# A gated mix of linear attention and softmax attention: Strassen groups over eight banks instead of six, v's split weights loaded back piece by piece, and kv's first weights loaded one per unit of v

## The chip, the cores and the metric

One NeuronCore of a Trainium2 chip runs the whole program. The metric is the device time of one execution in microseconds (us); lower is better. Five engines work side by side: PE (TensorE) does the matrix products and writes its sums to eight PSUM banks of 128 x 512 fp32; DVE (VectorE), ACT (ScalarE) and POOL (GpSimd) read and write banks and on-chip tiles; SP (SyncE) does nothing but issue transfers between memory and on-chip tiles. Each engine takes its instructions strictly in the order written, and waits at an instruction until all that it needs is there.

## The reference

Two attention blocks of 32 heads of 32 columns each see the same x (2048 rows, 1024 columns). A is linear attention, B is softmax attention, and a gate per row mixes them:

```
phi = lambda t: where(t > 0, t + 1, exp(t)) + 1e-6
A:  q, k, v = x @ A_wqkv         pq, pk = phi(q), phi(k)
    kv = pk^T v   z = sum(pk)    o = (pq kv) / (pq z + 1e-6)     a = o @ A_wo
B:  q, k, v = x @ B_wqkv         p = softmax(q k^T / sqrt(32))   b = (p v) @ B_wo
g = sigmoid(sum(x * gate_w))
result = g * a + (1 - g) * b
```

## The kernel before

**Three products for one.** A fp32 product is made of three faster ones. A tile t is split into a high part (ACT copies t into the fast type, L294) and a low part (DVE or POOL subtracts the high part from t, L295). The helper `three` then adds hi x hi (L153), hi x lo (L156) and lo x hi (L158) into one bank. So a line L153 in the profile is the first matmul of a triple and is the one that waits when a bank isn't free; L156 is the first that needs a low part.

**The stages.** B's v, q and k come first. The 2048 rows of x are four column blocks of x transposed, taken as two pairs, J = 0 and J = 1. For each pair:

- *v's pass*, `v_pass(J, k, banks)`: half of v's columns for the pair's 1024 rows. All eight banks are open at once, one for each 128 rows; for k = 0..7 every bank gets one triple. At the end ACT copies the eight banks out (L358, `v_out`).
- *Eight Strassen groups*, `quad(J, f, side)`: each makes 256 columns of q or k for the pair, as seven products of 12 matmuls. A product goes to the next bank of a ring of `NQB` banks. The products are read like this: ACT copies product 0 to P1 (L467); DVE adds product 1 to it (L469); products 2, 3 and 4 stay in their banks until DVE has product 4, and then L476, L477 and L478 read products 4, 3 and 2 in this order; L482 and L483 read product 5; L486 reads product 6. Each of the four results is split (`store`) and its two parts go to memory (`qk_d`), issued by SP. Between the steps, `quad` calls `next(side)`: one step each of the work that goes beside it. This is `quad_weights` (sums of q's and k's weights for the next group and their split), `late_side`, `spill_rest` (split parts of x put aside in memory, `xs`), and `wo_parts` (the output weights, on POOL and its own queue, L502 to L531).

In the first pair, v's split weights lie in places of the ring `RINGW`, which the groups' weights then overwrite. So `store_wv` puts them into memory (`wv_d`), and `load_wv_again` brings them back for J = 1, in the last group of J = 0 (`change`). The other side work of `change` is the split of the next pair's x, whose tiles are loaded by `load_pair`.

During v's pass the sums and differences of x blocks that Strassen's scheme needs are made by DVE (`sides`, L375 to L378), into tiles that held the groups' results and from which the stores to `qk_d` were made.

**After the groups** (from 417 us) comes a plan: a table `T` of each engine's expected time decides which work is written next. The function `linear` writes chunks in units of 24 matmuls (one 128-row tile, k = 0..7, in `three`). The first chunk is the other half of B's v, 16 units; then come chunks of A's k and v together ("kv"), then q and o. Beside them run the softmax heads: maxima of scores (matmuls L1232, L1237 on DVE), scores and exponentials (L1374, L1377), products with v (L1524), to the end. A chunk's weights are loaded by `load_w` into raw tiles, put in the queue `coming_w`, and split into place by `split_w` (L839 is its ACT cast). For the chunk that follows, the first `LEAD_W` = 5 weights are loaded in the last unit but one (t == NT - 2).

**Queues.** Every transfer made by `dma` is issued by SP (L170), in the order written. A transfer that waits for a tile to become free, or for one to be written, holds all that are written behind it.

Of the kernel before, what the change touches and what calls it, by code (L numbers as in the profile page):

```python
# [21 lines left out]
C = 512  # L22
# [3 lines left out]
LEAD_W = 5  # L26
# [23 lines left out]
def kernel(  # L50
# [31 lines left out]
    def f32(ap):  # L82
        return ap.bitcast(F32)
# [83 lines left out]
    def dma(to, of):  # L167

        T["sp"] = max(T["sp"], T["pe"]) + DMA_ISSUE
        nc.sync.dma_start(to, of)  # L170
# [140 lines left out]
    for side in PLACES:  # L311
        side["X12"] = side["T4"]
    NQB = 6
    RINGW = [(16, 0), (16, 1), (17, 0), (17, 1), (19, 0), (19, 1), (14, 0), (14, 1), (20, 0), (20, 1), (15, 0),
# [313 lines left out]

    V_BANKS = [list(range(8)), [6, 7, 2, 3, 4, 5, 0, 1]]
    raws_q = [raw_a, raw_b]  # L630
# [5 lines left out]

    def load_wv_again(ks):
        for k in ks:
            for p in range(2):
                dma(f32(ring_w(v_ring(1, k), p)), wv_d[k][:, p * C:(p + 1) * C])  # L640

# [31 lines left out]
    for k in range(NK):  # L673
# [5 lines left out]
        if k + 4 < NK:  # L679
            load_block(k + 4)  # L680
        v_pass(0, k, V_BANKS[0], range(TPC) if k == 0 else None)
        if k % 2:
# [19 lines left out]
    load_quad(raw_b, 1)  # L702
    for t, to in zip((0, 1, 6, 2, 3, 4, 5, 7), v_outs[0]):
        v_out(0, t, bank[V_BANKS[0][t]], to)

    def change():

        load_wv_again(range(NK - 2))
        split_x(raw_x1[0], 1, 0, 0)
        yield  # L710
        load_wv_again([NK - 2])
        split_x(raw_x1[0], 1, 1, 0)
        yield
        load_wv_again([NK - 1])
        split_x(raw_x1[0], 1, 0, 1)
        yield
        split_x(raw_x1[0], 1, 1, 1)
        yield
        split_x(raw_x1[1], 1, 0, 2)
        split_x(raw_x1[1], 1, 1, 2)  # L720
        yield
        split_x(raw_x1[1], 1, 0, 3)
        split_x(raw_x1[1], 1, 1, 3)
        yield

    quads(0, lambda: load_pair(raw_x1[0], 1, 0), spill_rest(0), parts)
    load_pair(raw_x1[1], 1, 1)
    quad(0, QUADS - 1, change())
    for k in range(NK):
        v_pass(1, k, V_BANKS[1])  # L730
        if k == 0:
# [31 lines left out]
    for t, to in enumerate(v_outs[1]):  # L763
        v_out(0, 2 * TPC + t, bank[V_BANKS[1][t]], to)

# [270 lines left out]
    def linear():  # L1036
        extra = iter(())
        for n, (i, t) in enumerate(units):
# [18 lines left out]
            for k in range(NK):  # L1057
# [37 lines left out]
                if follow and t == NT - 2 and k == 0:  # L1095
                    yield lambda: None if mix_here or stores else 0.0
                if follow and t == NT - 2 and k < min(LEAD_W, NK):
                    coming_w.append(load_w(*follow, k, LEAD_W + 1))
# [819 lines left out]
```

## Time and profile before

| | |
|---|---|
| median of 3 runs | 2833.21 us (2830.22 to 2836.54) |
| the profiled execution | 2832.33 us, its span 2830.3 us, granted clock 0.997 |
| PE from 540 us to the end | 2282.73 us busy of 2290.30 |

The profile describes one execution. A busy share says how long an engine had something in hand, not whether anyone waited for it; what the end hangs on is seen where PE waits and for whom. These are the stages of the span: length, then busy time and number of matmuls or instructions of PE, PE's weight loads, DVE, ACT and POOL, then the granted TensorE clock (1.00 is full), the busy share of the DMA engines and the GB/s that they moved.

```profile
0.00:51.00 51.00, 49.89 (x217) 41.58 (x218) 40.07 (x66) 28.50 (x51) 0.71 (x6) 1.00 0.93 298
51.00:211.40 160.40, 153.01 (x664) 124.98 (x662) 134.70 (x168) 56.01 (x117) 89.89 (x122) 0.99 0.91 287
211.40:259.00 47.60, 46.54 (x192) 37.69 (x192) 36.19 (x57) 20.18 (x36) 0.00 (x0) 0.94 0.79 250
259.00:417.00 158.00, 153.88 (x674) 126.16 (x675) 121.67 (x173) 59.46 (x115) 54.53 (x70) 1.00 0.79 253
417.00:540.00 123.00, 117.41 (x519) 94.94 (x518) 63.77 (x94) 38.60 (x66) 52.37 (x58) 0.99 0.87 270
540.00:2830.30 2290.30, 2282.73 (x13619) 1618.51 (x13617) 1934.73 (x3189) 1435.88 (x2713) 1905.68 (x895) 1.00 0.48 137
```

The rows are v's first pass, the first pair's groups, v's second pass, the second pair's groups, v's chunk, and all the rest.

### The profile page before, as it was taken

What the parts mean: (1) busy time and instruction counts of PE and PEld (TensorE: products, weight loads), DVE (VectorE), ACT (ScalarE), POOL (GpSimd) and SP (SyncE); (2) the same over time, 40 slices, a digit from 0 to 9 for tenths busy, and PEclk for the clock granted to TensorE, in tenths of its full rate; (3) what the DMA queues carried; (4) which work ended last, traced back from release to release, by engine and by line L of the source; (5) the groups of instructions that cost most, each with busy time, mean ns of one, the idle gap of its engine ahead of it and who ended that gap; (6) DMA issues with size and microseconds to landing.
All of it is one profiled execution on the core that took longest, in us unless ns stands there. A gap on an engine that the chain in (4) does not pass through costs nothing.

```text
span 2830.3 us, 47031 instructions
## 1 busy us (share of the span) xinstructions
PE 2803.5 (99%) x15880; PEld 2043.9 (72%) x15880; DVE 2331.1 (82%) x3745; ACT 1638.6 (58%) x3095; POOL 2103.2 (74%) x1150
## 2 busy tenths in 40 slices
PE   9999999999999999999999999999999999999999
PEld 8877788777776777667776777776676667666687
DVE  7886874788888888888888888888887888886688
ACT  5334332566676667666765666666666666666522
POOL 0660524599999998999899998989889988888000
PEclk9999999999999999999999999999999999999999
DMA  8997979633343434333433344556575554544774
GB/s 277 303 291 241 290 220 284 192 98 100 101 126 104 102 102 128 100 94 98 133 94 105 99 126 137 155 162 183 174 214 164 146 157 140 150 120 139 253 238 153
DMA packets 403340, 459.52 MB, mean 162 GB/s; under 512 B 106894, under 2 KB 234894, under 8 KB 401308
## 3 DMA queue, kind: packets, MB, share of 16 engines
q1 hardware_dynamic: 381084, 419.03, 48.7%
q0 software_dynamic: 22016, 37.50, 6.1%
q8 instruction: 126, 2.06, 0.3%
q14 instruction: 114, 0.93, 0.1%
HBM read 314.31 MB, written 127.66 MB: 156 GB/s over the span
## 4 chain that ended last, share of the span: by engine, by line
PE 85%; DMA 1%; issue 0%; DVE 0%; SPq 0%; ACT 0%; ACTq 0%; DVEq 0%
PE bank L1374 17%; PE bank L1232 16%; PE bank L1524 16%; PE bank L153 11%; PE bank L158 11%; PE bank L156 11%; PE bank L1296 1%; PE bank L1021 1%; PE bank L910 0%; DMA big<-ra 0%; DMA xh<-xs 0%; PE bank L1288 0%; SPq L170 0%; DMA big<-xs 0%; DMA extra<-in_a_wqkv 0%
## 5 line engine op out<-in xcount | busy, mean ns | idle before, releaser
L1459 POOL TENSOR_TENSOR big<-big,big 128x512 f32<-128x512 f32 (+2 forms) x694 | 1642.0, 2370 | 107.2 <-ACT big L1377 64.2
L1237 DVE TENSOR_REDUCE mx<-bank 128x1 f32<-128x512 f32 x2048 | 1314.6, 684 | 302.2 <-PE bank L1232 298.8
L1377 ACT ACTIVATE big<-bank 128x512 f32<-128x512 f32 x2048 | 1180.3, 602 | 429.6 <-PE bank L1374 364.1
L1374 PE MATMUL bank<-big,big 128*128 128x512 f32 x1888 | 741.7, 394 | 1.7 <-DMA big<-ml 1.7
L1232 PE MATMUL bank<-big,big 128*128 128x512 f32 x1888 | 739.6, 392 | 1.4 <-ACT big L1377 1.4
L153 PE MATMUL bank<-big,big 128*128 128x512 f32 x1576 | 619.1, 393 | 14.9 <-DVE mid L478 6.4
L156 PE MATMUL bank<-big,big 128*128 128x512 f32 x1576 | 617.0, 392 | 2.3 <-DVE big L295 1.8
L158 PE MATMUL bank<-big,big 128*128 128x512 f32 x1572 | 615.7, 392 | 0.0
L1524 PE MATMUL bank<-big,mid 128*32 128x512 f32 x4096 | 454.2, 593 | 0.0
L1374 PEld LDWEIGHTS bank<-big,big 128*128 128x128 f32 x1888 | 354.2, 188 | 125.9 <-issue 49.7
L1232 PEld LDWEIGHTS bank<-big,big 128*128 128x128 f32 x1888 | 354.6, 188 | 75.4 <-ACT big L1377 3.1
L153 PEld LDWEIGHTS bank<-big,big 128*128 128x128 f32 x1576 | 297.3, 189 | 83.8 <-issue 9.2
L156 PEld LDWEIGHTS bank<-big,big 128*128 128x128 f32 x1576 | 297.2, 189 | 65.5 <-DVE big L295 2.9
L158 PEld LDWEIGHTS bank<-big,big 128*128 128x128 f32 x1572 | 296.4, 189 | 64.5 <-DVE big L295 1.7
L1524 PEld LDWEIGHTS bank<-big,mid 128*32 128x32 f32 x4096 | 143.6, 110 | 264.4 <-issue 264.1
L1475 DVE TENSOR_TENSOR bank<-bank,big 128x512 f32<-128x512 f32 x364 | 252.2, 693 | 5.3 <-ACT big L1377 2.9
L294 ACT CAST big<-mid 128x512 fp32r<-128x512 f32 (+1 forms) x157 | 92.8, 618 | 116.2 <-DVE mid L1643 66.0
L295 DVE TENSOR_TENSOR big<-mid,big 128x512 fp32r<-128x512 f32 (+1 forms) x157 | 122.9, 799 | 43.9 <-ACT big L294 43.7
L1455 POOL TENSOR_TENSOR big<-big,big 128x1536 f32<-128x1536 f32 (+1 forms) x31 | 123.1, 3972 | 41.7 <-ACT big L1377 41.5
L153 PE MATMUL bank<-big,xh 128*128 128x512 f32 x376 | 147.2, 392 | 1.2 <-DMA xh<-xs 1.2
L158 PE MATMUL bank<-big,xh 128*128 128x512 f32 x376 | 147.0, 391 | 0.0
L156 PE MATMUL bank<-big,xh 128*128 128x512 f32 x376 | 146.8, 391 | 0.0
(163 smaller groups left out, 2122.9 us busy)
## 6 DMA issues: line engine op xcount, KB each, us to landing
big<-xs SPq DMA_DIRECT2D x288, 256.0 KB
big<-qk SPq DMA_DIRECT2D x690, 64.0 KB
xh<-xs SPq DMA_DIRECT2D x144, 256.0 KB
qk<-mid SPq DMA_DIRECT2D x128, 256.0 KB
big<-oA SPq DMA_DIRECT2D x84, 256.0 KB
xs<-big SPq DMA_DIRECT2D x64, 256.0 KB
oA<-mid SPq DMA_DIRECT2D x64, 256.0 KB
big<-big POOLq DMA_DIRECT2D x50, 256.0 KB, 5.8
```

The lines of the kernel that those rows point to most:

```text
L153: yield nc.tensor.matmul(ps, sh, mh_, start=(kt == 0), stop=False)
L156: yield nc.tensor.matmul(ps, sh, ml_, start=False, stop=(late and last))
L158: yield nc.tensor.matmul(ps, sl, mh_, start=False, stop=last)
L295: eng.tensor_sub(lo, src, f32(hi))
L1232: nc.tensor.matmul(bank[b], q[:, t % TPC * P:(t % TPC + 1) * P], k[:, j * C:(j + 1) * C], start=True, stop=True)
L1237: nc.vector.tensor_reduce(m[:, t, j:j + 1], bank[b], AX.X, ALU.max)
L1374: nc.tensor.matmul(bank[b], k[:, t * P:(t + 1) * P], q_cols(h, j), start=True, stop=True)
L1377: nc.scalar.activation(pr_t[i][:, j * C:(j + 1) * C], bank[b], AF.Exp, scale=SCALE)
L1455: nc.gpsimd.tensor_add(lacc[:, :qp], pr(0)[:, :qp], pr(1)[:, :qp])
L1459: nc.gpsimd.tensor_add(lacc[:, sl], lacc[:, sl], pr(t)[:, sl])
L1475: nc.vector.tensor_add(lacc[:, qp:] if t == NT - 1 else l_b[:, :n], l_b[:, :n], src)
L1524: nc.tensor.matmul(av_b[j * DH:(j + 1) * DH, :], v[:, t, :], pr(t)[:, j * C:(j + 1) * C], start=(t == 0), stop=(t == NT - 1))
```

## The change

Three edits, which leave what is computed as it is.

1. `NQB` is 8 instead of 6, and both of v's passes use the banks 0 to 7 in their order; `V_BANKS` goes. With six banks the last group of J = 0 ended in bank 1, and the second pass was given the order 6, 7, 2, 3, 4, 5, 0, 1; with eight it ends in bank 7. The first pass's banks are copied out in the order 0 to 7 instead of 0, 1, 6, 2, 3, 4, 5, 7.
2. v's split weights come back one place k at a time. A new stream `reload_wv` beside the groups waits for (8 - 2) x 7 + 1 = 43 steps and then loads k = 0 to 5, one per step, from group 6's second product on. `change` loads the last two. Before, `change` loaded k = 0 to 5 at group 7's first step, then k = 6, then k = 7.
3. After a chunk of v, the first five weights of the next chunk (kv) are loaded one in each of the units t = 10 to 14, at k = 0, instead of all five within t = 14, at k = 0 to 4.

```diff
-    NQB = 6
+    NQB = 8
...
-    V_BANKS = [list(range(8)), [6, 7, 2, 3, 4, 5, 0, 1]]
...
-    def load_wv_again(ks):
-        for k in ks:
-            for p in range(2):
-                dma(f32(ring_w(v_ring(1, k), p)), wv_d[k][:, p * C:(p + 1) * C])
+    def load_wv_again(k):
+        for p in range(2):
+            dma(f32(ring_w(v_ring(1, k), p)), wv_d[k][:, p * C:(p + 1) * C])
+
+    def reload_wv():
+
+        for _ in range((QUADS - 2) * NP + 1):
+            yield
+        for k in range(NK - 2):
+            load_wv_again(k)
+            yield
...
-    for t, to in zip((0, 1, 6, 2, 3, 4, 5, 7), v_outs[0]):
-        v_out(0, t, bank[V_BANKS[0][t]], to)
+    for t, to in enumerate(v_outs[0]):
+        v_out(0, t, bank[t], to)
 
     def change():
 
-        load_wv_again(range(NK - 2))
+        load_wv_again(NK - 2)
         split_x(raw_x1[0], 1, 0, 0)
         yield
-        load_wv_again([NK - 2])
+        load_wv_again(NK - 1)
         split_x(raw_x1[0], 1, 1, 0)
         yield
-        load_wv_again([NK - 1])
         split_x(raw_x1[0], 1, 0, 1)
...
-    quads(0, lambda: load_pair(raw_x1[0], 1, 0), spill_rest(0), parts)
+    quads(0, lambda: load_pair(raw_x1[0], 1, 0), reload_wv(), spill_rest(0), parts)
...
-        v_pass(1, k, V_BANKS[1])
+        v_pass(1, k, range(8))
...
-                if follow and t == NT - 2 and k < min(LEAD_W, NK):
+                if follow and kind == "v":
+                    if k == 0 and 0 <= t - (NT - 1 - LEAD_W) < LEAD_W:
+                        coming_w.append(load_w(*follow, t - (NT - 1 - LEAD_W), LEAD_W + 1))
+                elif follow and t == NT - 2 and k < min(LEAD_W, NK):
                     coming_w.append(load_w(*follow, k, LEAD_W + 1))
```

On PE, DVE, ACT and POOL the order of the instructions stays, but for ACT's copies of the first pass; it is the bank in each that changes. DVE in the second pair's first group, before (bank_238 to bank_245 are the banks 0 to 7; mid_226, mid_235 and mid_234 are P1, W2 and U2):

```order
L476 TENSOR_TENSOR mid_234<-bank_238,mid_226 128x512
L477 TENSOR_TENSOR mid_235<-bank_243,mid_234 128x512
L478 TENSOR_TENSOR mid_226<-bank_242,mid_235 128x512
L295 TENSOR_TENSOR mid_226<-mid_226,mid_232 128x512
L295 TENSOR_TENSOR big_222<-mid_225,big_222 128x512
L482 TENSOR_TENSOR mid_235<-bank_239,mid_235 128x512
L483 TENSOR_TENSOR mid_234<-bank_239,mid_234 128x512
```

And now:

```order
L476 TENSOR_TENSOR mid_234<-bank_242,mid_226 128x512
L477 TENSOR_TENSOR mid_235<-bank_241,mid_234 128x512
L478 TENSOR_TENSOR mid_226<-bank_240,mid_235 128x512
L295 TENSOR_TENSOR mid_226<-mid_226,mid_232 128x512
L295 TENSOR_TENSOR big_222<-mid_225,big_222 128x512
L482 TENSOR_TENSOR mid_235<-bank_243,mid_235 128x512
L483 TENSOR_TENSOR mid_234<-bank_243,mid_234 128x512
```

The group's products lay in the banks 2, 3, 4, 5, 0, 1, 2 and now lie in 0 to 6, so that the bank read by L478 is taken again eight products later and not six.

SP around the first pair's groups 6 and 7 (qk_... are the stores of a group's results, of which `_134` to `_143` belong to group 6 and `_150` to `_158` to group 7; wv_252 to wv_259 are v's split weights for k = 0 to 7; in_xT is x for the next pair):

```order
 L170 DMA qk_0_6_134<-mid_230 128x512
 L170 DMA qk_1_6_142<-mid_236 128x512
+L170 DMA big_614<-wv_252 128x512 x2
+L170 DMA big_221<-wv_253 128x512 x2
+L170 DMA big_221<-wv_254 128x512 x2
 L170 DMA qk_0_6_134<-mid_232 128x512
 L170 DMA qk_1_6_142<-mid_226 128x512
+L170 DMA big_222<-wv_255 128x512 x2
```

```order
 L170 DMA mid_228<-in_xT 128x512
-L170 DMA big_614<-wv_252 128x512 x2
-L170 DMA big_221<-wv_253 128x512 x2
-L170 DMA big_221<-wv_254 128x512 x2
-L170 DMA big_222<-wv_255 128x512 x2
-L170 DMA big_222<-wv_256 128x512 x2
-L170 DMA big_223<-wv_257 128x512 x2
+L170 DMA big_223<-wv_258 128x512 x2
 L170 DMA qk_0_6_150<-mid_230 128x512
 L170 DMA qk_1_6_158<-mid_236 128x512
-L170 DMA big_223<-wv_258 128x512 x2
```

Twelve loads went from between the x tiles and group 7's first stores to places among group 6's stores, ahead of the x tiles.

SP at the end of v's chunk (v_161 is a store of a finished unit, xs_ and xh are x put aside before and loaded again, in_a_wqkv are kv's weights):

```order
 L170 DMA big_210<-xs_3_82 128x512
 L170 DMA v_161<-mid_234 128x512
+L170 DMA mid_225<-in_a_wqkv 128x256 x2
```

```order
 L170 DMA big_210<-xs_7_86 128x512
 L170 DMA v_161<-mid_234 128x512
-L170 DMA mid_225<-in_a_wqkv 128x256 x2
+L170 DMA mid_229<-in_a_wqkv 128x256 x2
 L170 DMA mid_233<-in_xT 128x512
-L170 DMA extra<-in_a_wqkv 128x256 x2
-L170 DMA mid_227<-in_a_wqkv 128x256 x2
 L170 DMA big_210<-xs_7_70 128x512
 L170 DMA big_210<-xs_7_86 128x512
-L170 DMA mid_228<-in_a_wqkv 128x256 x2
 L170 DMA zrep<-in_xT 128x512
-L170 DMA mid_229<-in_a_wqkv 128x256 x2
```

The first weight (mid_225) now stands four units earlier, the other three that went from here one unit apart behind it; the fifth (mid_229) stays in the last unit but one.

More of the change, by code (lines that the diff above doesn't have):

```diff
@@ L680 @@
             load_block(k + 4)
-        v_pass(0, k, V_BANKS[0], range(TPC) if k == 0 else None)
+        v_pass(0, k, range(8), range(TPC) if k == 0 else None)
         if k % 2:
@@ L763 @@
     for t, to in enumerate(v_outs[1]):
-        v_out(0, 2 * TPC + t, bank[V_BANKS[1][t]], to)
+        v_out(0, 2 * TPC + t, bank[t], to)
     def load_v1(raws, ks):
```

## The prediction

> **What bounds the kernel now.** I read the page first, then the list of PE's waits, then the stretches in which those waits lie. The page says that the span is matmuls:
>
> ```profile
> span 2830.3 us, 47031 instructions
> PE 2803.5 (99%) x15880; PEld 2043.9 (72%) x15880; DVE 2331.1 (82%) x3745; ACT 1638.6 (58%) x3095; POOL 2103.2 (74%) x1150
> ```
>
> The change takes no matmul away, so it can win only what PE stands still or runs slowly. The list of waits (total us, times, longest) begins with these:
>
> ```profile
> PE bank L153 <- DVE mid L478: 6.4, 5, 2.5
> PE bank L153 <- DMA big<-xs: 3.2, 1, 3.2
> ```
>
> The rows quoted below place these and the next longest ones: all lie before 540 us, in the Strassen groups, between them and v's pass, and where v's chunk hands over to kv. What comes after 540 us is bound by PE itself, so what is won before reaches the end. The waits also cost clock. Windows (length, busy us and matmuls of PE, and so on; the granted clock is the third number from the right):
>
> ```profile
> 51.50:70.50 19.00, 19.00 (x85) 15.76 (x84) 12.25 (x20) 8.21 (x15) 1.25 (x2) 1.00 0.67 216
> 190.10:193.50 3.40, 3.12 (x7) 2.48 (x8) 2.67 (x3) 1.23 (x3) 3.30 (x5) 0.50 0.41 152
> 214.00:217.40 3.40, 3.40 (x9) 2.63 (x9) 2.90 (x5) 1.83 (x4) 0.00 (x0) 0.50 1.05 391
> 528.00:531.50 3.50, 3.50 (x11) 2.69 (x10) 1.38 (x2) 1.86 (x3) 0.45 (x1) 0.51 0.91 306
> ```
>
> At full clock 3.40 us hold 85 x 3.40/19.00 = 15 matmuls, at half clock 9: a slow stretch loses 6 x 0.224 = 1.4 us. There are four (two lie together, from 210.6). Each follows a wait of 2.5 us or more; after the shorter ones the clock stayed. So the most there is to win is 2830.3 - 2803.5 = 26.8 us of standing still and 5.6 us of clock.
>
> **Part 1: the eight banks.** A group is 84 matmuls, 19.0 us for PE. The five waits for L478 say that DVE reads product 2 late. The question is whether DVE is late because PE is, or by itself. The longest of DVE's own waits from 62 to 217 us, and L478 and PE at the start:
>
> ```profile
> DVE mid L295 <- ACT mid L294: 16.1, 22, 0.7
> L478 DVE TENSOR_TENSOR mid<-bank,mid x16: 691/691/692, 68.2 to 413.0; 128x512 f32<-128x512 f32 x16
> 51.03 0.39 PE L153 MATMUL bank<-big,big 128*128 128x512 f32 x1
> ```
>
> DVE waits there for ACT casts of DVE's own results, and for PE not once. Through the first pair's groups DVE sets its own pace: L478 comes at 68.2 us in group 0 and at 209.89 in group 7 (row below), 20.2 us apart on average against PE's 19.0. More banks cannot hurry it; they let PE run ahead until something else of DVE's stops it. That is the weights. DVE and PE around group 7 and the pass behind it:
>
> ```profile
> 189.55 0.69 DVE L478 TENSOR_TENSOR mid<-bank,mid 128x512 f32<-128x512 f32 x1
> 192.53 2.46 DVE L295 TENSOR_TENSOR big<-mid,big 128x512 fp32r<-128x512 f32 x1
> 193.13 1.30 POOL L531 TENSOR_TENSOR zrep<-zrep 128x512 f32<-128x512 f32 x1
> 209.89 0.69 DVE L478 TENSOR_TENSOR mid<-bank,mid 128x512 f32<-128x512 f32 x1
> 211.31 0.69 DVE L295 TENSOR_TENSOR mid<-mid,mid 128x512 fp32r<-128x512 f32 x1 [0.73 <-ACT mid L294]
> 216.35 0.69 DVE L486 TENSOR_TENSOR mid<-bank,mid 128x512 f32<-128x512 f32 x1
> 225.73 0.69 DVE L378 TENSOR_TENSOR mid<-xh 128x512 f32<-128x512 f32 x1 [5.22 <-DMA qk<-mid]
> 190.38 0.77 PE L153 MATMUL bank<-big,big 128*128 128x512 f32 x1 [2.53 <-DVE mid L478]
> 208.12 0.39 PE L158 MATMUL bank<-big,big 128*128 128x512 f32 x1
> 211.47 0.76 PE L153 MATMUL bank<-big,big 128*128 128x512 f32 x1 [2.96 <-DMA big<-wv]
> 219.59 0.39 PE L153 MATMUL bank<-big,big 128*128 128x512 f32 x1
> ```
>
> With eight banks PE, which begins group 0 at 51.03, starts group 7 at about 51.0 + 7 x 19.0 = 184 us and its product 2 two products, 5.4 us, later. The low half of that product's weights is the split at 192.53, done at 195.0. PE waits there instead, and has 10 matmuls and four products left (2.3 + 10.9 us): it ends the group at 208.2, where before it ended at 208.5 (the row at 208.12). I count the first pair's bank waits at nothing, then; their bounds go into the next sum.
>
> The split at 192.53 takes 2.46 us where the other DVE rows here take 0.69; POOL's subtraction `L531 zrep<-zrep` runs inside it. The Trainium skill, "SBUF — State Buffer", section "SBUF: two separate sides", says that a DVE instruction with two SBUF operands and a GpSimd one lock each other out of a shared port for the whole instruction. The trace agrees (2.46 against 0.69 us), and by that rule no number of banks shortens this chain.
>
> **Part 2: v's weights come back earlier.** The sixteen loads now issue from 204.5 us on, behind group 6's stores:
>
> ```profile
> 201.13 3.25 SPq L170 DMA_DIRECT2D mid<-in_xT  x4
> L170 SPq DMA_DIRECT2D big<-wv x16: 319/320/2086, 204.5 to 219.8; - x16
> 168.60:189.00 20.40, 19.26 (x85) 15.60 (x84) 18.59 (x21) 6.40 (x14) 13.04 (x18) 1.00 0.99 314
> 189.00:204.00 15.00, 13.62 (x53) 11.07 (x54) 12.24 (x14) 5.58 (x12) 10.01 (x14) 0.89 0.69 233
> 210.00:226.00 16.00, 14.03 (x50) 11.09 (x51) 9.13 (x15) 5.70 (x10) 0.00 (x0) 0.79 1.04 383
> ```
>
> Twelve of them move into 183 to 201 us. The last two columns (DMA share, GB/s) say that the stretch to 189 is full and the next has room. 12 x 0.262 MB at the 383 GB/s of the last row are 8.2 us of transfers. SP issues them one place per step, each right behind the product that frees its place, and PE, being ahead, has run that product. So the 2.96 + 0.50 us go. Next in line stands DVE: v's pass over k = 0 goes through banks 0 to 7, and banks 3, 6 and 7 hold group 7's products that L478, L483 and L486 read. L486 ends at 216.35 + 0.69 = 217.04, so the last bank of k = 0 starts at 217.1 where it started at 219.59: 2.5 us. PE comes to it through about 2 us of idling, near what halved the clock before; I put one slow stretch at one chance in two, 0.7 us. **Term 1: 2.5 - 0.7 = 1.8 us**; bounds -0.3 (two slow stretches) and 2.5.
>
> The Trainium skill, "TensorE: Matmul & The Clock Gate", section "HAM oscillation — how this bites in real kernels", lets the clock fall only after idling for a window of about 3.4 us. Here 2.53 us sufficed (0.50 in the row from 190.10), so the measurement decides; by the rule term 1 would be 2.5 us.
>
> The same loads did a second harm. Group 7's stores of q and k stood on SP behind them, and DVE's L378 (the row at 225.73), which overwrites a stored tile, waited 5.22 us. With the loads out of the way that store can go when its split is done (211.31 + 0.69 = 212.0) and L378 can run at 220.5. Behind it hang all of the pass's side matrices, the loads for them, ACT's copies of v and the split of T4 in the second pair's first group, so this chain comes 5.2 us earlier. PE itself comes 1.8 earlier, and so its waits on that chain go:
>
> ```profile
> 259.39 0.50 PE L153 MATMUL bank<-big,big 128*128 128x512 f32 x1 [0.88 <-ACT mid L358]
> 277.35 0.50 PE L156 MATMUL bank<-big,big 128*128 128x512 f32 x1 [1.07 <-DVE big L295]
> 279.75 0.50 PE L156 MATMUL bank<-big,big 128*128 128x512 f32 x1 [0.77 <-DVE big L295]
> 322.41 0.47 PE L153 MATMUL bank<-big,big 128*128 128x512 f32 x1 [0.44 <-DVE mid L478]
> 343.18 0.47 PE L153 MATMUL bank<-big,big 128*128 128x512 f32 x1 [1.45 <-DVE mid L478]
> 341.00:361.00 20.00, 18.55 (x83) 15.03 (x82) 16.46 (x26) 7.86 (x14) 0.00 (x0) 1.00 0.77 244
> ```
>
> **Term 2: 0.88 + 1.07 + 0.77 = 2.7 us**; bounds 0 (the chain stays where it is; then term 1 is swallowed too) and 2.7. The changed bank order alone also lets the first product follow the first of ACT's copies, not the third.
>
> **Term 3**: the second pair's bank waits, 0.44 + 1.45 = **1.9 us**. Here DVE has room (16.46 busy of 20.00 us), and two more products, 5.4 us, cover a lateness of 1.45. Bounds 0 (it comes back as a wait for weights, as in group 7) and 1.9.
>
> **Part 3: kv's first weights.** Where v's chunk ends:
>
> ```profile
> 520.33 0.99 SPq L170 DMA_DIRECT2D mid<-in_a_wqkv  x2
> 521.74 0.80 SPq L170 DMA_DIRECT2D big<-xs  x2
> 526.82 0.50 PE L153 MATMUL bank<-big,big 128*128 128x512 f32 x1 [3.24 <-DMA big<-xs]
> 536.77 0.62 ACT L839 CAST big<-extra 128x512 fp32r<-128x512 f32 x1 [0.99 <-DMA extra<-in_a_wqkv]
> 537.94 0.51 PE L1232 MATMUL bank<-big,big 128*128 128x512 f32 x1 [1.44 <-ACT big L1377]
> 480.00:512.00 32.00, 32.00 (x151) 26.69 (x150) 24.35 (x37) 11.07 (x20) 11.95 (x11) 1.00 0.89 274
> 516.00:537.00 21.00, 17.26 (x67) 12.97 (x65) 9.73 (x13) 7.60 (x13) 5.52 (x5) 0.92 0.91 296
> ```
>
> PE waits for x that SP issued behind kv's weights; then ACT's cast of the last weight waits for its load, an exponential stands behind the cast, and PE wants the exponential's bank. Of the ten loads of 0.131 MB that stand here together, eight move into the four units before (one pair stays). At 296 GB/s these are 0.44 us each. Eight moving out shorten the queue ahead of the last weight by 3.5 us, so PE resumes 3.5 earlier than 537.94. **Term 4: 3.5 us**, the two waits shrinking and the slow stretch at 528 going. Bounds 0 (the queue is as full in the units before, 0.89) and 3.24 + 1.44 + 1.4 = 6.1.
>
> Sum: 1.8 + 2.7 + 1.9 + 3.5 = 9.9 us. The profiled execution took 2832.33 us (its span 2830.3 and 2.0 around it), 0.9 below the median shown, within its runs' range. 2832.3 - 9.9 = **2822.4 us**.
>
> **Rivals.** *The chain behind L378 stays.* If the early loads make DVE or POOL wait elsewhere, all before 280 us stays DVE's: 1.9 + 3.5 = 5.4, 2826.9 us. For it: the full DMA before 189 us. Against it: room from 189 on. *kv's queue only moves.* With 0.89 in the units before, x comes late there: terms 1 to 3, 6.4, 2825.9 us. For it: 8 x 0.44 = 3.5 us of loads against 32 x 0.11 = 3.5 us of room. Against it: a pair of loads, 0.9 us, comes once per unit of 24 matmuls, 24 x 0.224 = 5.4 us. *The change does not do what it says*: every bank wait turns into a weight wait, in the second pair too, and the chain stays: 3.5 us, 2828.8. *Slower*: the twelve loads queue ahead of the four x tiles (the row at 201.13) that are split in group 7. Were their 8.2 us of transfers passed on whole, L486 would end at 225.2, PE be 5.6 late and 1.4 slower in clock, less terms 2 and 3 (4.6), and with kv's queue moved only: 2832.3 + 2.4 = 2834.7 us. It decides when those tiles land after 212 us, where DVE now splits them, behind the row at 211.31; they are issued from 201 on, and 189 to 204 has 15 x (1 - 0.69) = 4.6 us of room, so I hold it unlikely.
>
> **How the numbers follow.** The forecast 0.56, the first rival 0.13, the second 0.13, the third 0.10, slower 0.08. Its own bounds run from 2818 (term 4 at 6.1, no slow stretch) to 2826; with 3 us either way, the spread of the runs before, and the rivals' 2827 to 2829, the range is 2814 to 2830. A measurement of this kernel can tell 0.2%, 5.7 us, from no change: faster than 2827.5 are the forecast, the second rival and half of the first, 0.76; slower than 2838.9 is half of the slower case, where further waits join it, 0.04; no change is the rest, 0.20.
>
> **What would show it.** No wait for L478 by PE in the second pair; in the first pair a wait for L295 near 190 us in place of it, and PE at v's pass near 208 us as now. No wait for wv; waits for banks near 210 to 217. L378 without its 5.2 us, and none of the three waits between 259 and 280. Near 515 to 530 a wait for x under 2 us and a granted clock of 1.00. I am wrong if PE reaches the pass well before 208 us (then DVE followed PE after all), or if waits for xs appear between 480 and 515.

## The result: 6.9 us faster

| | before | changed |
|---|---|---|
| median | 2832.2 us (8 runs, 2827.87 to 2836.54) | 2825.31 us (8 runs, 2821.66 to 2829.28) |
| ratio | | 0.9977, 95% interval 0.9967 to 0.9988 |
| profiled execution | 2832.33 us, span 2830.3 | 2824.52 us, span 2822.7 |

The interval is a gain of 3.4 to 9.3 us. The forecast was 2822.4 us, 9.9 us faster than the profiled execution before; that one and the profiled one after are 7.8 apart.

The page of the changed kernel, first its span and the engines' busy time, and then the list of PE's waits (total us, times, longest):

```profile
span 2822.7 us, 47003 instructions
PE 2801.9 (99%) x15880; PEld 2043.3 (72%) x15880; DVE 2330.5 (83%) x3745; ACT 1638.2 (58%) x3095; POOL 2104.1 (75%) x1150
```

```profile
PE bank L153 <- DVE mid L486: 3.9, 1, 3.9
PE bank L153 <- DMA xh<-xs: 2.4, 2, 1.7
PE bank L153 <- ACT big L294: 2.3, 3, 1.2
PE bank L1382 <- DMA big<-ml: 2.2, 2, 1.6
PE bank L153 <- DVE mid L483: 1.5, 1, 1.5
PE bank L1240 <- ACT big L1385: 1.1, 1, 1.1
...
PE bank L153 <- DMA big<-xs: 1.0, 1, 1.0
PE bank L153 <- DVE mid L478: 0.4, 1, 0.4
```

The waits for L478 fell from 6.4 to 0.4 us and those for `wv` are gone. New on the list are L483 and L486, DVE's reads of the last two products of group 7: the next in line. (L1240, L1382 and L1385 are the lines 1232, 1374 and 1377 of before.)

Where the lead came from is best read by setting the start of the same matmul in both traces side by side. Both hold all 15880, so the nth of one is the nth of the other:

| place (us before) | PE's lead | gained there | forecast |
|---|---|---|---|
| v's second pass, 225, behind the slow stretch | 1.0 | 1.0 | 1.8 (term 1) |
| after the three waits, 280 | 4.6 | 3.6 | 2.7 (term 2) |
| after the second pair's bank waits, 343 | 6.9 | 2.3 | 1.9 (term 3) |
| start of v's chunk, 440 to 460 | 5.8 | -1.1 | 0 |
| v's chunk to kv, 577 | 9.4 | 3.6 | 3.5 (term 4) |
| the two places at 2081 and 2606 | 7.3 | -2.1 | 0 |

The four terms came to 10.5 us where 9.9 were forecast, and 3.2 were given back at places that the forecast counted at nothing. The pass's beginning in the changed kernel; PE, then DVE and POOL:

```profile
204.66 0.39 PE L153 MATMUL bank<-big,big 128*128 128x512 f32 x1
207.25 0.50 PE L153 MATMUL bank<-big,big 128*128 128x512 f32 x1 [0.39 <-DVE mid L478]
211.08 0.50 PE L153 MATMUL bank<-big,big 128*128 128x512 f32 x1 [1.49 <-DVE mid L483]
215.95 0.80 PE L153 MATMUL bank<-big,big 128*128 128x512 f32 x1 [3.90 <-DVE mid L486]
212.27 3.03 DVE L295 TENSOR_TENSOR big<-mid,big 128x512 fp32r<-128x512 f32 x2
215.22 0.68 DVE L486 TENSOR_TENSOR mid<-bank,mid 128x512 f32<-128x512 f32 x1
219.41 0.69 DVE L378 TENSOR_TENSOR mid<-xh 128x512 f32<-128x512 f32 x1
212.86 1.27 POOL L537 TENSOR_TENSOR zrep<-zrep 128x512 f32<-128x512 f32 x1
```

PE enters the pass at 204.66, 6.8 us ahead of before, waits for none of v's weights, and then stands 5.8 us for DVE. L486 ends at 215.9, where 217.0 was expected. L378 has no wait ahead of it and runs at 219.41 (220.5 was expected). Two splits of x take 3.03 us instead of 1.3, with POOL's subtraction inside them. (POOL works on on-chip tiles alone here: none of its instructions in the trace before reads or writes a bank, as the list of engines at the start might suggest.) The clock behind the wait (windows as in the prediction; third number from the right):

```profile
211.20:214.60 3.40, 0.85 (x3) 0.36 (x3) 3.40 (x2) 0.97 (x2) 3.09 (x5) 1.00 1.06 408
214.61:221.44 6.83, 5.49 (x13) 4.33 (x14) 6.00 (x11) 2.38 (x4) 0.39 (x1) 0.50 0.65 231
528.63:532.05 3.42, 3.42 (x9) 2.64 (x9) 3.00 (x8) 1.91 (x4) 0.00 (x0) 0.50 0.55 183
```

The slow stretch that was put at one chance in two did come, and the one at 528 stayed.

### The profile page after: what moved, and what is told of

It reads as the page before. It is cut to its first block, busy times and chain, and to the rows that moved or that the text cites. A ratio compares the mean times of both kernels' runs of the same rounds, so it can differ in the third digit from the quotient of the medians.

```text
span 2822.7 us, 47003 instructions
## 1 busy us (share of the span) xinstructions
PE 2801.9 (99%) x15880; PEld 2043.3 (72%) x15880; DVE 2330.5 (83%) x3745; ACT 1638.2 (58%) x3095; POOL 2104.1 (75%) x1150
## 4 chain that ended last, share of the span: by engine, by line
PE 90%; DMA 2%; issue 1%; DVE 0%; ACT 0%; SPq 0%; ACTq 0%; DVEq 0%
PE bank L1382 17%; PE bank L1240 16%; PE bank L1532 16%; PE bank L153 13%; PE bank L156 13%; PE bank L158 13%; PE bank L1304 1%; PE bank L1026 1%; PE bank L915 0%; DMA big<-ra 0%; DMA xh<-xs 0%; SPq L170 0%; PE bank L1296 0%; DMA qk<-mid 0%; DVE big L295 0%
## 5 line engine op out<-in xcount | busy, mean ns | idle before, releaser
L1385 ACT ACTIVATE big<-bank 128x512 f32<-128x512 f32 x2048 | 1179.6, 602 | 433.7 <-PE bank L1382 368.4
L1382 PE MATMUL bank<-big,big 128*128 128x512 f32 x1888 | 742.4, 394 | 2.2 <-DMA big<-ml 2.2
L1240 PE MATMUL bank<-big,big 128*128 128x512 f32 x1888 | 739.8, 392 | 1.1 <-ACT big L1385 1.1
L153 PE MATMUL bank<-big,big 128*128 128x512 f32 x1576 | 618.1, 392 | 9.2 <-DVE mid L486 3.9
L158 PE MATMUL bank<-big,big 128*128 128x512 f32 x1572 | 614.9, 391 | 0.5 <-DMA big<-xs 0.2
L1382 PEld LDWEIGHTS bank<-big,big 128*128 128x128 f32 x1888 | 354.5, 188 | 127.3 <-issue 48.1
L1240 PEld LDWEIGHTS bank<-big,big 128*128 128x128 f32 x1888 | 355.0, 188 | 75.0 <-ACT big L1385 2.4
L153 PEld LDWEIGHTS bank<-big,big 128*128 128x128 f32 x1576 | 296.9, 188 | 77.6 <-ACT big L294 4.5
L158 PEld LDWEIGHTS bank<-big,big 128*128 128x128 f32 x1572 | 295.8, 188 | 65.9 <-DVE big L295 3.0
L295 DVE TENSOR_TENSOR big<-mid,big 128x512 fp32r<-128x512 f32 (+1 forms) x157 | 122.2, 795 | 44.6 <-ACT big L294 44.2
L294 ACT CAST big<-mid 128x512 fp32r<-128x512 f32 (+1 forms) x157 | 92.8, 618 | 113.1 <-DVE mid L1651 66.0
L153 PE MATMUL bank<-big,xh 128*128 128x512 f32 x376 | 147.1, 391 | 2.4 <-DMA xh<-xs 2.4
L158 PE MATMUL bank<-big,xh 128*128 128x512 f32 x376 | 146.9, 391 | 0.0
```

Of the source, the lines that this page charges most:

```text
L153: yield nc.tensor.matmul(ps, sh, mh_, start=(kt == 0), stop=False)
L158: yield nc.tensor.matmul(ps, sl, mh_, start=False, stop=last)
L295: eng.tensor_sub(lo, src, f32(hi))
L1240: nc.tensor.matmul(bank[b], q[:, t % TPC * P:(t % TPC + 1) * P], k[:, j * C:(j + 1) * C], start=True, stop=True)
L1382: nc.tensor.matmul(bank[b], k[:, t * P:(t + 1) * P], q_cols(h, j), start=True, stop=True)
L1385: nc.scalar.activation(pr_t[i][:, j * C:(j + 1) * C], bank[b], AF.Exp, scale=SCALE)
```

## The experiments

The theory after the result: edits 1 and 2 let PE run ahead in the first pair, but DVE is late there by itself, because POOL slows it; so PE's waits only change their names until DVE has room, in the second pair. Edit 3 is a gain of its own. Rivals: the banks are worth their 6.4 us of waits; DVE's lateness is its own work; the queue at v's end only moves. Each time below is a median beside that of the kernel before on the same chip.

### One edit at a time

The first takes the kernel before and makes edit 1 alone:

```diff
-    NQB = 6
+    NQB = 8
...
-    for t, to in zip((0, 1, 6, 2, 3, 4, 5, 7), v_outs[0]):
+    for t, to in enumerate(v_outs[0]):
```

> The kernel before with the eight banks and the two bank orders alone. Theory: PE runs ahead in the first pair's groups but v's weights still issue in group 7's first step, so PE waits for them at the second pass and is no further than before at 222 us (0 to -1 us); L378 keeps its wait of about 5 us, the waits for L295 at 277 and 280 us stay; the copies' order takes the 0.9 us at 259 and the second pair's bank waits go (1.7 to 2.5). Total -2 to -4 us. Rival: the bank waits are worth what the list of waits gives them, -6.4 us or more.

Measured: 2827.83 us beside 2831.89, ratio 0.9989 (0.9978 to 1.0). PE's waits from 51 to 212 us, and the longest wait behind them:

```profile
PE bank L158 <- DVE big L295: 2.3, 3, 1.2
PE bank L153 <- ACT big L294: 2.0, 3, 0.8
...
PE bank L153 <- DMA big<-wv: 4.4, 1, 4.4
```

With eight banks there is no wait for a bank in the first pair, and 4.3 us of waits for weights in their place (L153 needs the high part of a product's weights, ACT's cast, and L158 the low part, DVE's subtraction; both come late from DVE's chain): the exchange that part 1 of the prediction described, here as large as what it replaced (4.5 us before). Then PE waits for `wv`, as expected. In the first pair the banks are thus worth nothing, which speaks against the rival's 6.4 us; the interval alone, up to 6.2 us, would barely do so. In the second pair there is no wait for a bank any more, as expected, though L378 still has its wait (5.9 us). The 0.9 us that the order of ACT's copies was to take at 259 us stayed (1.0).

The second makes edit 2 alone, with six banks:

```diff
-        load_wv_again(range(NK - 2))
+        load_wv_again([NK - 2])
...
-    quads(0, lambda: load_pair(raw_x1[0], 1, 0), spill_rest(0), parts)
+    quads(0, lambda: load_pair(raw_x1[0], 1, 0), reload_wv(), spill_rest(0), parts)
```

> The kernel before with the piecewise load of v's split weights alone (six banks). Theory: PE does not wait for these weights any more (3.5 us) but then for L483 and L486, so it is 1 to 2.5 us ahead at 222 us; L378 loses its wait of 5.2 us and with it the two waits at 277 and 280 us go (1.8); the second pair's bank waits stay (1.9) and may grow. Total -3 to -4.5 us. Rival: the loads are early only because eight banks let PE run ahead; with six they come late again and the gain is under 1 us.

Measured: 2830.57 us, ratio 0.9999 (0.999 to 1.0009): nothing, where 3 to 4.5 us were expected. The rival's number came (under 1 us) but not its reason: the weights did come in time. PE's waits from 51 to 225 us:

```profile
PE bank L153 <- DVE mid L478: 7.3, 5, 2.0
PE bank L153 <- DVE mid L486: 2.9, 1, 2.9
PE bank L153 <- DVE mid L483: 1.9, 1, 1.9
```

The whole of the 3.5 us came back as waits for L483 and L486, and in this execution more: PE was 3.7 us behind at 222 us. What made L486 end 4.5 us later than before is seen in group 7, on ACT and then on DVE:

```profile
203.18 0.59 ACT L467 COPY mid<-bank 128x512 f32<-128x512 f32 x1 [4.32 <-DMA qk<-mid]
204.32 0.69 DVE L295 TENSOR_TENSOR big<-mid,big 128x512 fp32r<-128x512 f32 x1 [4.44 <-ACT big L294]
```

ACT's copy of product 0 overwrites a tile from which a result of group 6 is stored, and waits for that store; before, it did not wait. The edit puts the loads of `wv` among these stores: this one was issued at 197.1 us and took 6.0 us to land, where such stores near 200 us take 3.0 to 3.7 in the kernel before, the first and the third run (one read in each), which load the weights later. The same copy waits 1.9 us in the fourth run and 4.5 in the seventh, both with this edit, and not at all in the changed kernel's trace. So edit 2 has a price that the prediction did not count; how often it falls due is not known.

From 222 to 417 us PE waited for nothing, with six banks. So the second pair's 1.9 us of bank waits, booked as term 3, are not the price of six banks alone: they come when PE is ahead of DVE, and go when it is not. Either edit alone removes them.

The third makes edit 3 alone:

```diff
-                if follow and t == NT - 2 and k < min(LEAD_W, NK):
+                if follow and kind == "v":
+                    if k == 0 and 0 <= t - (NT - 1 - LEAD_W) < LEAD_W:
+                        coming_w.append(load_w(*follow, t - (NT - 1 - LEAD_W), LEAD_W + 1))
+                elif follow and t == NT - 2 and k < min(LEAD_W, NK):
```

> The kernel before with the five kv weights one per unit alone. Theory: the waits of 3.2 and 1.4 us near 527 and 538 us shrink by 3.5 us, nothing else moves: -3.5 us. Rival: the queue only moves: waits for x appear between 440 and 520 us and the gain is under 1.5 us.

Measured: 2826.97 us, ratio 0.9984 (0.9973 to 0.9995). Its only wait near v's end, and the windows from 512 to 540 us before and with this edit:

```profile
525.07 0.50 PE L153 MATMUL bank<-big,big 128*128 128x512 f32 x1 [0.66 <-DMA big<-xs]
```

```profile
512.00:540.00 28.00, 23.32 (x97) 18.12 (x97) 15.42 (x23) 11.91 (x21) 9.44 (x8) 0.94 0.76 249
```

```profile
512.00:540.00 28.00, 27.27 (x122) 21.71 (x121) 22.23 (x35) 16.46 (x30) 11.87 (x9) 1.00 0.76 243
```

4.7 us of standing became 0.7 and the slow stretch went, and the DMA share in the window did not change (0.76). Between 440 and 470 us PE stood 1.2 us for x (0.9 before), so the queue did not merely move, and the rival falls. By its own medians this is 4.9 us of the change's 6.9; the intervals of the three edits are too wide to be added up, but edit 3 is the only one whose interval, taken alone, leaves out no change.

### What makes DVE late

The fifth and sixth take POOL's work on the output weights out of the first pair, before and with the change. It is done in and behind the second pair, so that their totals mean nothing:

```diff
-    quads(0, lambda: load_pair(raw_x1[0], 1, 0), spill_rest(0), parts)
+    quads(0, lambda: load_pair(raw_x1[0], 1, 0), spill_rest(0))
...
     quad(1, QUADS - 1, beside(leave(), parts))
+    for _ in parts:
+        pass
```

> The kernel before, with POOL's work on the output weights taken out of the first pair's groups (it runs in the second pair's and right behind them, so only the first 259 us are read). Theory: DVE is late there because 24 to 29 of its some 170 instructions between 51 and 211 us take 1 to 2.5 us instead of 0.7 beside POOL's, some 25 us in all. Without POOL none takes over 0.9 us, L478 comes every 19 us, PE does not wait once for L478 and ends the first pair's groups near 204 us, and then waits for v's weights, which are issued as late as before. Rival: DVE is late by its own work and its waits for ACT; waits for L478 of 3 us or more stay.

Measured: PE waits for nothing at all from 51 to 245 us. The largest group of L295 between 51 and 211 us (count, busy, mean ns, then idle before it), first before, then here:

```profile
L295 DVE TENSOR_TENSOR big<-mid,big 128x512 fp32r<-128x512 f32 x39 | 38.5, 1004 | 10.0 <-ACT big L294 10.0
```

```profile
L295 DVE TENSOR_TENSOR big<-mid,big 128x512 fp32r<-128x512 f32 x44 | 29.3, 686 | 11.6 <-ACT big L294 11.6
```

DVE's longest wait for PE there (62 to 217 us), and the loads of `wv` by their line (first and last start):

```profile
DVE mid L476 <- PE bank L158: 12.8, 6, 3.4
```

```profile
L170 SPq DMA_DIRECT2D big<-wv x16: 319/320/1321, 188.8 to 202.9; - x16
```

The mean fell from 1004 to 686 ns, and now DVE waits for PE (12.8 us). PE enters the pass at 201.8 us and is 13.0 us ahead at 222. One thing was expected otherwise: with six banks and the one block of loads, the wait for `wv` went as well. The block issues from 188.8 us instead of 204.5, because the stores ahead of it on SP are ready earlier. So the wait that edit 2 removes was POOL's doing too. This rules out the rival that DVE's own work makes it late.

The edit also takes POOL's transfers out of the first pair, so these might be the cause instead. The windows from 51 us to the end of group 7's L486, before and here, hold the same 176 DVE instructions:

```profile
51.00:217.04 166.04, 158.07 (x675) 128.71 (x674) 140.20 (x176) 58.58 (x121) 89.89 (x122) 0.97 0.91 290
51.00:205.19 154.19, 154.19 (x682) 127.69 (x681) 112.26 (x176) 57.50 (x103) 1.25 (x2) 1.00 0.74 232
```

DVE is busy 27.9 us less, its waits for ACT are much the same (26.7 and 29.2 us in all), and it waits for a transfer in neither. So it is the length of DVE's instructions beside POOL's that makes it late, not the transfers.

> The changed kernel with the same taken out (again the first 259 us are read). Theory: no wait for a bank or a weight in the first pair's groups; L486 of group 7 comes 4 us or more earlier than the 215.2 us of the changed kernel, the waits for L478, L483 and L486 at the pass's first k fall from 5.8 us to under 3, and the clock stays full behind them: PE is 3 to 5 us further at 230 us than in the changed kernel. Rival: L486 hangs on the x tiles and their split, which POOL does not touch: the waits at the pass stay over 5 us.

Measured: no wait from 51 to 245 us here either; group 7's L486 starts at 203.94 us (215.22 in the changed kernel) and PE is 12.6 us ahead of the changed kernel at 222 us, where 3 to 5 were expected. Without POOL, the kernel before and the changed one differ by less than 1 us there.

### Where to put POOL's work

The eighth spreads POOL's pieces thinner in the first pair and thicker in the second, in the changed kernel:

```diff
-            at[0] += PIECE_STEP
+            at[0] += 4.6 if at[0] < 52 else 3.1
```

> The changed kernel with POOL's pieces of the output weights spread otherwise: one every 4.6 steps in the first pair's groups and one every 3.1 in the second pair's, instead of one every 3.4 throughout. Theory: some 8 us less of slowed DVE work in the first pair; the weight waits in the groups go, L486 comes 1 to 3 us earlier, and PE is 1 to 4 us further at 230 us; the second pair has room for it (DVE 122 of 158 us busy, eight banks). Total -1 to -3 us. Rival: the second pair's DVE becomes late instead, waits appear between 277 and 417 us, and the time stays or rises.

Measured: 2818.14 us (4 runs) beside 2830.92, ratio 0.9945 (0.9928 to 0.9961), clear of the changed kernel's interval. PE at the pass:

```profile
209.79 0.79 PE L153 MATMUL bank<-big,big 128*128 128x512 f32 x1 [3.66 <-DVE mid L483]
212.43 0.79 PE L153 MATMUL bank<-big,big 128*128 128x512 f32 x1 [0.99 <-DVE mid L486]
```

No wait in the first pair's groups; at the pass 4.7 us for DVE, and 4.4 us further than the changed kernel at 222. The rival's part is there as well: 3.1 us of waits for weights between 336 and 360 us, with a slow stretch behind them, took that lead back in this execution. It was the slowest of the four, so where the median's gain lies is not shown. Nor was this spread run in the kernel before, without the three edits.

The ninth and tenth put fewer pieces into the first pair and some six into v's second pass, where POOL did nothing, before and with the change:

```diff
-            at[0] += PIECE_STEP
+            at[0] += 7.0 if at[0] < 50 else 3.5
...
         v_pass(1, k, range(8))
+        for _ in range(3 if k else 0):
+            next(parts, None)
```

> The kernel before, with POOL's pieces of the output weights spread anew: one every 7 steps in the first pair's groups, some six in v's second pass (three steps per k from k = 1 on, where POOL was idle), one every 3.5 steps in the second pair's groups. Theory: POOL's slowing of DVE is what all waits up to the second pass come from, the late return of v's weights too. So with six banks and the weights loaded back in one block, PE is already 6 to 10 us further at 230 us, as far as the whole change brought it or further; the second pair, with six banks, gets some of it back as waits for L478. Total -5 to -8 us. Rival: banks and the early return of the weights are needed for it; -3 us or less.

> The changed kernel with the same spread of POOL's pieces. Theory: PE is 5 to 9 us further at 230 us than in the changed kernel; the second pass has room for the pieces, the second pair's groups about as many as before; 4 to 7 us reach the end, more than with the lighter first pair alone (2818 us). Rival: POOL's pieces in the second pass slow DVE there, and the pass or the work behind it becomes late: no better than 2818 us.

Measured: 2836.87 us beside 2832.77 (ratio 1.0013, 1.0004 to 1.0023) and 2830.22 (0.9989, 0.9978 to 1.0). By their times the rivals were right: the ninth is slower than the kernel before, the tenth slower than the changed kernel by its median (the intervals overlap). By its reason only the tenth's was: the ninth's held that banks and early weights are needed, but without them PE was 13 us ahead at 222 us, as with no POOL at all. Then, at the start of the second pair, in that run, with ACT ahead of it:

```profile
242.11 0.63 ACT L294 CAST big<-mid 128x512 fp32r<-128x512 f32 x1 [6.94 <-DMA mid<-in_b_wqkv]
247.20 0.62 ACT L294 CAST big<-xh 128x512 fp32r<-128x512 f32 x1 [4.47 <-DMA xh<-in_b_wqkv]
256.21 0.80 PE L153 MATMUL bank<-big,big 128*128 128x512 f32 x1 [10.67 <-ACT mid L358]
```

PE stands 10.67 us for ACT's copies of v, which stand behind casts of the next groups' weights, which wait for their transfers. Two more waits, for low parts from DVE at 278 and 282 us (6.0 us), and the slow stretches with all three made it 4.7 us of lateness at 284. In the tenth the first wait is 8.16 us, and one of 4.41 follows at 276. The transfers are late mostly because DVE frees their tiles later: this is the first of them on SP, in the ninth run and then in the fifth, where PE enters the pass at the same time and POOL is silent in it:

```profile
238.01 0.38 SPq L170 DMA_DIRECT2D mid<-in_b_wqkv  x1
227.10 0.38 SPq L170 DMA_DIRECT2D mid<-in_b_wqkv  x1
```

Both times SP has been standing for a split of DVE's (L295). From 215 to 235 us DVE is busy 19.14 us for 23 instructions in the ninth and 16.26 for 26 in the fifth.

### Smaller pieces, and all that held together

The fourth moves the splits of x for k = 2 and 3 from group 7 to behind the pass's k = 0, in the changed kernel:

```diff
-        split_x(raw_x1[1], 1, 0, 2)
-        split_x(raw_x1[1], 1, 1, 2)
         yield
-        split_x(raw_x1[1], 1, 0, 3)
-        split_x(raw_x1[1], 1, 1, 3)
...
         if k == 0:
+            for kk in (2, 3):
+                for jj in range(2):
+                    split_x(raw_x1[1], 1, jj, kk)
             sides(raw_x1[0], 0)
```

> The changed kernel, with the splits of x for k = 2 and 3 taken out of group 7 and put behind the second pass's k = 0. Theory: in the changed kernel PE stands 5.8 us for DVE's L478, L483 and L486 at the pass's first k, and loses about 2.4 us of clock after that; L486 is late because DVE splits four x tiles ahead of it. Without them L486 comes about 3 us earlier, the wait for it falls under 1.5 us and the clock stays full: PE is 4 to 5.5 us further at 222 us than in the changed kernel, and 3 to 5 us of it reach the end (about 2820 us). Rival: what is moved is missing later, at k = 2 of the pass or at L378 and the work behind it, and the time stays within 1 us of the changed kernel's.

Measured: 2822.45 us beside 2831.89, ratio 0.9965 (0.9954 to 0.9976), against 0.9977 for the changed kernel: the intervals overlap. At the pass PE waits only for L486, 0.5 us where it was 5.8 in all, as expected. But in this profiled execution the groups ahead held 4.9 us of waits for weights and two slow stretches, so PE was only 0.3 us further at 222 us, where 4 to 5.5 were expected. It shows the place, not the size.

The seventh moves kv's five weights one unit earlier (t = 9 to 13):

```diff
-                    if k == 0 and 0 <= t - (NT - 1 - LEAD_W) < LEAD_W:
+                    if k == 0 and 0 <= t - (NT - 2 - LEAD_W) < LEAD_W:
...
```

> The changed kernel with kv's five weights one unit earlier still, in the units t = 9 to 13. Theory: what is left at v's end (1.1 us at 527 us for an exponential that stands behind ACT's cast of the last weight, and a slow stretch behind it, 1.4 us) goes, since the last load is no longer there: -1 to -2.5 us. Rival: the transfers between 440 and 520 us are full as they are, the loads make x late in an earlier unit: no gain, or 1 us slower.

Measured: 2820.59 us beside 2830.92, ratio 0.9962 (0.9947 to 0.9976), again overlapping. The wait that was to go is still there, and what stands ahead of it on ACT:

```profile
526.54 0.62 ACT L844 CAST big<-extra 128x512 fp32r<-128x512 f32 x1 [1.30 <-DMA extra<-in_a_wqkv]
527.71 0.51 PE L1240 MATMUL bank<-big,big 128*128 128x512 f32 x1 [1.13 <-ACT big L1385]
```

The cast that holds the exponential (L844, which is L839 of before) is of one of the weights loaded after the five. My theory of this wait fell; the better time is not explained by it. In the traces the seventh run is 4.0 us ahead of the changed kernel at the end, of which 3.0 came behind 577 us, at waits that scatter.

The eleventh is the tenth with the edits of the fourth and seventh:

> The same, and besides it the splits of x for k = 2 and 3 behind the second pass's k = 0 (as in the fourth run) and kv's five weights one unit earlier (as in the seventh). Theory: the three act at different places; with POOL out of the way the splits bring little (1 us), the weights 1 to 2 us: 2815 us or a little less, the fastest of all. Rival: the splits moved into the pass meet POOL's pieces there, and it is no faster than without them.

Measured: 2828.37 us beside 2832.77, ratio 0.9978 (0.9966 to 0.999), where 2815 were expected: at the pass's end PE waits as in the tenth (7.2 us for ACT's copies). The twelfth takes the eighth's spread instead, with POOL silent in the pass:

> The changed kernel with three of the edits tried: POOL's pieces as in the eighth run (none in v's second pass), the splits of x for k = 2 and 3 behind the pass's k = 0, kv's weights one unit earlier. Theory: the pieces are worth what the eighth run showed (2818 us), the splits take what is left of the wait for L486 (1 us) since POOL is silent in the pass, the weights bring little or nothing (0 to 2): 2815 to 2818 us, the fastest of all. Rival: the three compete for the same slack before the pass's end, and it is no faster than the eighth run, or slower by DVE's lateness in the second pair.

Measured: **2813.51 us** (2812.08 to 2816.28) beside 2833.26, ratio 0.9937 (0.9924 to 0.9951), the fastest of all by its median; the interval overlaps the eighth's. PE waits once between 51 and 225 us; from 259 to 417 it waits 3.0 us more, for weights (L294 and L295):

```profile
PE bank L153 <- DVE mid L486: 0.5, 1, 0.5
```

It is 11.4 us ahead of the changed kernel at 222 us and 8.3 at the end. The rival, that the three compete, did not come; that the two smaller edits add to the eighth is likely but not shown.

## Why the prediction was right, and where not

- **Part 1, the first pair's bank waits counted at nothing.** Right in its substance: the first experiment shows 4.3 us of weight waits where 4.5 of bank waits were. The picture drawn for it was of one execution: the split at 192.53 us does not meet POOL in every one. In the profiled changed kernel it took 0.68 us, the groups had 1.3 us of waits, and PE was at the pass at 204.7 us and not near 208. That is the sign by which the prediction called itself wrong ("I am wrong if PE reaches the pass well before 208 us (then DVE followed PE after all)"). What it was to tell of did not happen: DVE waited for PE in no place up to L486, which came only 1.1 us earlier while PE came 6.8 earlier.
- **Term 1.** Forecast 1.8, came 1.0. That L486 gates the pass once the weights are there held (215.9 against 217.0 expected), and the slow stretch came, over two windows instead of one. What this term took as fixed is when L486 comes. That hangs on how DVE's instructions meet POOL's (here two splits of 3.03 us), and on the store of group 6 that lands late among the loads: in the second experiment L486 came 4.5 us later and nothing of the 2.5 us was left. The rival "slower" had such a delay, but by x tiles, and not by a store.
- **Term 2.** L378 lost its 5.22 us, and the three waits at 259, 277 and 280 us went: 3.6 for 2.7. The trace agrees with each step; that early loads cause it is shown by the second experiment, where L378 ran without a wait too; in the first, without them, it kept 5.9 us. That the changed bank order alone takes the wait for ACT's copies is not borne out (1.0 us left in the first).
- **Term 3.** The size came (2.3 for 1.9). That it takes two more banks was too narrow: the first experiment has no such waits with eight banks, but neither has the second with six. They are DVE's lateness against PE's lead, and banks are one way to cover it.
- **Term 4.** Forecast 3.5, came 3.6, its size in part by luck: the slow stretch at 528, counted as gone, stayed in the changed kernel, and the two waits alone fell by 3.6 us (4.7 to 1.1). In the third experiment it went, and PE gained 5.6 us there (from 0.8 behind at 344 us to 4.8 ahead at 538).
- **"What comes after 540 us is bound by PE itself"** is the step that failed, with the beginning of v's chunk: 3.2 us of the 10.5 were given back there to waits for x and for the scores' row maxima. They are in every trace and scatter: at 440 to 470 us from 0.5 to 3.1 us over the twelve full traces, at 2081 from 0.3 to 1.7. The profiled execution before had little of both (0.9 and 0.4), the one after more (2.0 and 1.7). So it is not shown that the lead itself brings them about. The seventh run speaks against it: 10.2 us ahead of the kernel before at 538 us, it was 11.5 ahead at the end. The medians' 6.9 us, with an interval of 3.4 to 9.3, are nearer to 7.3 than to the forecast.

The Trainium skill, "SBUF — State Buffer", section "SBUF: two separate sides", was used for the split that took 2.46 us. The fifth experiment agrees: with POOL silent in the first pair L295's mean is 686 ns, beside POOL 1004. The reach of this slowing was larger than the prediction saw. It is behind the bank waits, the weight waits, the late return of `wv` and L378's wait at once (0.3 us of 5.22 are left there in the fifth).

## What to carry to other kernels

When several waits of the critical engine name several buffers, find the engine that is late for all of them, and what slows it, before giving any one more buffers or earlier loads: here two of three edits moved waits from bank to weight to the next read in the first pair, and a change of POOL's pace on top of them brought about as much again as all three (12.8 us by the medians beside 6.9). A lead won in one stage is worth only what the next stage's late engine leaves of it; where the slowing work goes decides, and an idle engine is not a free place for it (with six pieces in v's second pass a lead of 12.5 us over the changed kernel at 222 us was 7.0 us of lateness at 284). Spreading a block of loads one per unit, ahead of its use, paid for kv's weights: this was the one part whose gain came as forecast and showed alone. For `wv` the same idea alone brought nothing, since the loads came among stores for which another engine was waiting.

## What the runs showed of the hardware

**The clock falls by a raster.** In each execution all starts and ends of slow stretches lie at multiples of 3.41 us from one another (before: 190.12, 193.53, 210.60, 217.43, 528.04, 531.45: 1, 6, 8, 99 and 100 steps of 3.413 from the first). What counts is how long PE stood within one such window, not how long a wait was. Over the twelve full traces up to 700 us, all 28 windows with 1.9 us or more of standing were followed by half clock, of eight between 1.6 and 1.9 four, and below 1.6 one (windows that were slow already left out of the last two counts). So the same wait can cost a slow window, 1.4 us, or nothing, by where it falls: one of 1.97 us that ended at 197.6 us in the fourth run was followed by half clock, one of 1.97 us at 153.6 in the second, divided between two windows, was not. The exception is the changed kernel's window ahead of 528.63; beside it the seventh run's, which kept the clock:

```profile
525.20:528.60 3.40, 2.28 (x15) 1.72 (x14) 2.33 (x4) 2.12 (x5) 0.52 (x1) 1.00 0.31 108
```

```profile
526.72:530.13 3.41, 2.42 (x15) 2.17 (x16) 2.94 (x5) 2.38 (x6) 0.52 (x1) 1.00 0.28 83
```

Both hold eight matmuls of one column each beside the large ones (15 in all); why the one fell and not the other is open. The Trainium skill, "TensorE: Matmul & The Clock Gate", section "Part 1: The HAM clock gate (the "warmup" mystery)", says that the window is 3413 ns and free-running; the raster agrees. The same section's table lets the clock fall after an idle window of about 3.4 us; here less was enough: 1.9 of 3.41 us sufficed every time.

**DVE's pace varied by some 4 us in 100 between two executions** with the same instructions. Up to v's chunk the third experiment runs what the kernel before runs. By 168 us DVE's instructions had taken 4.4 us longer in sum there, with the same waits, and PE was 4.1 us later from 171 to 187 us (0.4 at 51). With POOL silent the fifth and the sixth agree (112.26 and 112.27 us busy for the same 176 instructions), so the likely reason is that POOL's and DVE's instructions meet otherwise in each execution.
